# Routing attention and SwiGLU on one core: one-hot copies through GpSimd, q/k transposes held per head pair, a later second batch, feed-forward ahead of preparation

## The chip, the cores and the metric

The kernel runs on one core of one Trainium2 chip. The metric is device time in microseconds (us). A core has TensorE (PE: matmuls; PEld is its weight load), VectorE (DVE), ScalarE (ACT), GpSimd (POOL) and the DMA queues of SyncE (SP), ScalarE and GpSimd. Each engine works through its own instructions in the order in which they were written.

## The reference

Attention in which a query sees only the keys of its own cluster, then a gated feed-forward. Cut to what matters:

```python
# q, k, v: (4, 8, 768, 64); centroids: (8, 16, 64)
q_assign = argmax(q_n @ c_n); k_assign = argmax(k_n @ c_n)     # per head, normalised
mask = q_assign[:, :, :, None] == k_assign[:, :, None, :]
attn = softmax(where(mask, q @ k.T / 8, -1e9)); y = attn @ v
x = y as (3072, 512)
xn = x / sqrt(mean(x * x) + 1e-6) * rms_g
out = (silu(xn @ w_gate) * (xn @ w_val)) @ w_out               # 512 -> 1536 -> 512
```

## The kernel before

The 32 (batch, head) pairs, numbered n, form eight groups g of four heads. The mask is folded into the matmul: to the 64 rows of q and k that each head has come 16 rows of a one-hot of its cluster, so that the 80-row product of kext and qext holds the score plus a large term where the clusters agree; the exponential takes that term off again.

To prepare a group (`group_work`), each head's q and k, staged side by side by DMA, are transposed on TensorE in two parts (`trans`, tile tq), copied by ScalarE to `qkT`, cast by GpSimd into qext (`qcast`) and by VectorE into kext (`kcast`), and v is cast by GpSimd into vbf (`vcast`). Then `scores_c`, called with m = 0 and 1 for the two halves of the sequence, multiplies with the centroids (tile sc); VectorE transposes, takes the maximum, compares and transposes back (tile oh), and eight small DMAs, two for each head, copy the one-hot rows from oh into qext and kext. `qkT` is one tile of four heads, in a pool of one buffer (`qk32`).

The work runs in eight units u, each half the queries of one batch: unit 0 and 1 are batch 0 (groups 0 and 1), 2 and 3 batch 1 (groups 2 and 3), and so on. For each of the eight heads h of a unit three pairs of score matmuls go to TensorE (`scores`), each followed by one exponential on ScalarE (tile pT), and `pv` accumulates the head before against v (tile acc, one PSUM buffer for two heads; VectorE's reciprocal and multiplication into x free it). Between these pieces the unit gives out its `fill`, a list of (cost, function) pairs, so that the costs given out keep pace with the unit's 24 score steps (6 in unit 0). In unit u >= 2 the fill is the out matmuls of unit u - 2, then gate and value matmuls of unit u - 1 mixed with the preparation of a later group. `rms(u - 1)` stands after the second score step of unit u: ScalarE's last squares, a chain of VectorE's, the normalised tile xn. `ffn_work` transposes xn (tile tx, line 310) and then goes through the gate and val products, 12 of each.

What the change touches:
- The start (lines 395 to 418). `t0(h)` transposes head h of group 0. With `early` set, ScalarE also casts each half of k from PSUM into kext, and the eight one-hot DMAs of group 0 are triggered by ScalarE, each set of four once its oh is there. Group 1's first two heads follow. The 8 warm matmuls at the beginning have a tile in the pool of the scores, `ps_s`.
- Unit 0 (line 441). Its fill is the rest of group 1's preparation (`first[4:]`) and then the loads of all weights, which GpSimd triggers.
- `second_batch` (lines 428 to 433), called in unit 0 after the head before head 6 has been accumulated. A tiny DMA `hold` makes SP wait for the latest reciprocal of that unit; the loads of q, k and v of batch 1 stand behind it.
- Unit 1 (lines 443 and 444). Its fill begins with six pieces of group 2 (three heads' transposes) and then mixes `ffn_work(0)` with the rest of groups 2 and 3.
- `gv` (lines 329 to 332). Tanh goes to a tile th, and VectorE's (th + 1) * gate to a second tile gu.

Of the kernel before, what the change touches and what calls it, by code (L numbers as in the profile page):

```python
# [9 lines left out]
F32 = mybir.dt.float32  # L10
# [3 lines left out]
ALU = mybir.AluOpType  # L14
ACT = mybir.ActivationFunctionType
# [3 lines left out]
ZS = 2048.0  # L19
# [3 lines left out]
def kernel(  # L23
# [12 lines left out]
    nc = tc.nc  # L36
    B, H, S, D = q.shape
# [3 lines left out]
    P = 128  # L41
# [3 lines left out]
    HG = 4  # L45
# [10 lines left out]
    pool = lambda n, b, **kw: ctx.enter_context(tc.tile_pool(name=n, bufs=b, **kw))  # L56
    const = pool("const", 1)
    stage = pool("stage", NQ)
    qk32 = pool("qk32", 1)
    asg = pool("asg", 1)  # L60
    ptp = pool("ptp", 3)
    xp = pool("xp", 1)
# [14 lines left out]
    def load_qk(n, kq=None):  # L77
        if n >= B * H:
            return
        staged[n] = stage.tile([P, ST, 2, D], F32, tag="qk", name="qk")  # L80
        nc.sync.dma_start(out=staged[n][:, :, 0], in_=src(q, n))
        (kq or nc.sync).dma_start(out=staged[n][:, :, 1], in_=src(k, n))
# [17 lines left out]

    warm = const.tile([P, 512], BF16)
    nc.vector.memset(warm, 1.0)
    warm_ps = ps_s.tile([P, 2, 512], F32, tag="s", name="warm")
    for i in range(WARM):
        nc.tensor.matmul(warm_ps[:, i % 2], lhsT=warm[:, :P], rhs=warm, start=True, stop=True)


    def rsqrt(ms, n):
# [13 lines left out]
        return y  # L122


    ones = const.tile([P, P], F32)
    nc.vector.memset(ones, 1.0)
    cnt = const.tile([P, 32], F32)
    nc.vector.tensor_tensor_scan(cnt, ones[:, 0:32], ones[:, 0:32], 0.0, op0=ALU.mult, op1=ALU.add)
    cntT = const.tile([P, 32], F32)
    nc.vector.transpose(cntT, cnt)  # L130
    ident_f = const.tile([P, P], F32)
# [48 lines left out]

    qkT = {}

    def trans(g, h, part, early=False):
        if (h, part) == (0, 0):
            qkT[g] = qk32.tile([P, HG, S], F32, tag="qkT", name="qkT")
        qk = staged[g * HG + h]
        ps = ps_g.tile([P, UQ], F32, tag="gen", name="tq")
        for i in range(HT):
            t = part * HT + i
            nc.tensor.transpose(ps[:, i * P:(i + 1) * P], qk[:, t].rearrange("p a d -> p (a d)"), ident_f)  # L190
        c = slice(part * UQ, (part + 1) * UQ)
        nc.scalar.copy(qkT[g][:, h, c], ps)  # L192
        if early:
            nc.scalar.activation(kext[g % 4][:D, h, c], ps[D:], ACT.Copy, scale=1.0 / ZS)

    def qcast(g, h):
        nc.gpsimd.tensor_copy(qext[g % 4][:D, h], qkT[g][:D, h])  # L197

    def kcast(g, h):
        nc.vector.tensor_scalar_mul(kext[g % 4][:D, h], qkT[g][D:, h], 1.0 / ZS)  # L200

    def vcast(n):
        nc.gpsimd.tensor_copy(vbf[n // HG % 4][:, n % HG, :, :D], stagedv[n])
# [8 lines left out]
    def scores_c(g, m, h0=0, h1=HG, early=False):  # L212
        if not early:
            ps = ps_g.tile([P, UQ], F32, tag="gen", name="sc")
        else:
            if m == 0:
                scps[g, h0] = ps_s.tile([P, 2, 512], F32, tag="s", name="sc")
            ps = scps[g, h0][:, m, :UQ]
        r = slice(32 * h0, 32 * h1)
        for h in range(h0, h1):  # L220
            nc.tensor.matmul(ps[32 * h:32 * h + 32], lhsT=cblk[:, g * HG % H + h],  # L221
                             rhs=qkT[g][:, h, m * UQ:(m + 1) * UQ], start=True, stop=True)
# [12 lines left out]
        nc.vector.transpose(oh[r, m * UQ:(m + 1) * UQ], ohT[r])  # L235
        if m:
            for h in range(h0, h1):
                q_ = nc.scalar if early else nc.sync
                q_.dma_start(out=qext[g % 4][D:D + NC, h], in_=oh[32 * h:32 * h + NC])
                q_.dma_start(out=kext[g % 4][D:D + NC, h], in_=oh[32 * h + NC:32 * h + 2 * NC])  # L240

# [73 lines left out]
    def gv(u, f, val):  # L315
        if f == 0 and not val:
            gvT[u] = xp.tile([P, FC, UQ], BF16, tag="gvT", name="gvT")
        w = wv if val else wg
        ps = ps_g.tile([P, UQ], F32, tag="gen", name="val" if val else "gate")
        for c in range(CC):  # L320
            nc.tensor.matmul(ps, lhsT=w[:, c, f * P:(f + 1) * P], rhs=xnT[u][:, c], start=c == 0, stop=c == CC - 1)  # L321
        last = u == NU - 1
        if not val:
            th = ffn.tile([P, UQ], F32, tag="th", name="th")
            if last:
                nc.scalar.activation(th, ps, ACT.Silu)
                gates[u] = th
            else:
                nc.scalar.activation(th, ps, ACT.Tanh, scale=0.5)  # L329
                gu = ffn.tile([P, UQ], F32, tag="gu", name="gu")  # L330
                nc.vector.scalar_tensor_tensor(gu, th, 1.0, ps, op0=ALU.add, op1=ALU.mult)  # L331
                gates[u] = gu
        elif last:
            nc.vector.tensor_mul(gvT[u][:, f], gates[u], ps)
        else:
            nc.vector.scalar_tensor_tensor(gvT[u][:, f], gates[u], 0.5, ps, op0=ALU.mult, op1=ALU.mult)  # L336
# [16 lines left out]
    def group_work(g):  # L353
        w = []
        for h in range(HG):
            n = g * HG + h
            w.append((0.25, lambda h=h: trans(g, h, 0)))

            def second(h=h, n=n):
                trans(g, h, 1)  # L360
                qcast(g, h)
                kcast(g, h)
                vcast(n)
                if g > 1:
                    load_qk(n + NQ)
                    load_v(n + NV)
            w.append((0.25, second))
        for m in range(2):
            w.append((0.7, lambda m=m: scores_c(g, m)))
        return w  # L370
# [23 lines left out]

    def t0(h):
        for part in range(2):
            trans(0, h, part, True)
        qcast(0, h)
        if NQ + h < H:
            load_qk(NQ + h)  # L400

    first = group_work(1)
    t0(0)
    centroids_t()
    t0(1)
    for n in range(2, H):
        load_v(n)
    nc.sync.dma_start(out=gcol, in_=moe_rms_g.rearrange("(c p) -> p c", p=P), allow_slow_non_contiguous=True)
    t0(2)
    for m in range(2):  # L410
        scores_c(0, m, 0, 2, True)
    t0(3)
    for m in range(2):
        scores_c(0, m, 2, 4, True)
    for h in range(HG):
        vcast(h)
    for _, f in first[:4]:
        f()

    def weights():  # L420
        for c in range(CC):
# [78 lines left out]
```

## Time and profile before

| | |
|---|---|
| median of 3 runs | 405.89 us (405.69 to 407.38) |
| profiled execution, its own time | 405.33 us |
| its span, first to last instruction | 403.4 us |
| mean granted clock of TensorE | 0.941 |
| busy: PE, PEld | 359.1 us (89%), 217.5 us (54%) |
| busy: DVE, ACT, POOL | 241.7 us (60%), 260.3 us (65%), 57.5 us (14%) |

By stage, from the trace's windows:

| us from the span's start | PE busy | ACT busy | DVE busy | PE clock |
|---|---|---|---|---|
| 0 to 20 | 10.69 | 8.82 | 10.04 | 0.97 |
| 20 to 40 | 14.30 | 11.13 | 12.92 | 0.69 |
| 40 to 60 | 14.85 | 14.06 | 1.51 | 0.57 |
| 60 to 80 | 10.82 | 8.01 | 8.75 | 0.59 |
| 80 to 100 | 18.92 | 14.72 | 13.66 | 0.99 |
| 100 to 120 | 19.68 | 16.03 | 13.47 | 1.00 |

The busy share of an engine is a mean over stages with different limits; the granted clock is a share of TensorE's full speed, and a matmul at half clock takes about twice as long, so a busy TensorE at 0.57 does little more than half of what it does at 1.00. Unit 0 runs from about 29 to 60 us, unit 1 from there to about 113.

### The profile page before, as it was taken

Reading aid. Unit: us, or ns where it says so; the run is one execution under the profiler, and the core shown is the slowest. Engines: PE = TensorE matmul, PEld = TensorE weight load, DVE = VectorE, ACT = ScalarE, POOL = GpSimd, SP = SyncE. Lnnn points to the kernel's source line nnn. Section 1 sums busy time; section 2 is a strip of 40 time slices with the busy share of each in tenths; the row PEclk is TensorE's granted clock in tenths of the full one; section 3 lists DMA queues with packets and bytes.
Section 4 is the critical chain, followed back from the end, with each engine's and each line's share of the span. In section 5 each row is a group of like instructions: output and inputs, shape, how many; then the busy total and the mean of one; then the engine's idle time right before and its main releaser. Section 6 shows DMA issues by size and latency. Waiting matters only on the chain.

```text
span 403.4 us, 7758 instructions
## 1 busy us (share of the span) xinstructions
PE 359.1 (89%) x3003; PEld 217.5 (54%) x3017; DVE 241.7 (60%) x556; ACT 260.3 (65%) x459; POOL 57.5 (14%) x84
## 2 busy tenths in 40 slices
PE   6458685589999999999998999899999999999896
PEld 3135344357645665566555664566556655664452
DVE  5457001686677678766865677566876646666432
ACT  5329584368875877678766876577767785784230
POOL 1149203203300320022101220031100000000000
PEclk9958655699999999999999999999999999999999
DMA  9923999954512432224222100200020002000102
GB/s 171 243 77 66 215 199 254 265 121 108 128 32 89 98 80 63 91 66 117 61 70 69 41 2 17 82 2 0 3 83 18 0 2 80 0 2 26 53 1 80
DMA packets 63877, 32.01 MB, mean 79 GB/s; under 512 B 53088, under 2 KB 59744, under 8 KB 63840
## 3 DMA queue, kind: packets, MB, share of 16 engines
q1 hardware_dynamic: 57712, 25.80, 25.7%
q0 software_dynamic: 2736, 4.72, 6.5%
q10 hardware_dynamic: 3392, 0.98, 1.3%
q8 instruction: 24, 0.39, 0.4%
q14 instruction: 13, 0.11, 0.1%
HBM read 28.35 MB, written 6.29 MB: 86 GB/s over the span
## 4 chain that ended last, share of the span: by engine, by line
PE 69%; DVE 9%; ACT 9%; DMA 7%; issue 3%; ACTq 1%; SPq 1%; DVEq 0%
PE gate L321 15%; PE val L321 14%; PE s L253 13%; PE o L345 9%; PE acc L269 8%; PE tq L190 5%; ACT pT L255 4%; ACT junk L288 3%; DMA out_dram<-o_sb 3%; PE sc L221 3%; DMA qk<-in_q_dram 2%; DMA qk<-in_k_dram 2%; DVE o_sb L348 1%; DMA kext<-oh 1%; PE tx L310 1%
## 5 line engine op out<-in xcount | busy, mean ns | idle before, releaser
L255 ACT ACTIVATE pT<-s,off 128x768 bf16<-128x768 f32 x192 | 171.4, 901 | 57.7 <-PE s L253 57.5
L253 PE MATMUL s<-qext,kext 80*128 80x384 bf16 x384 | 98.8, 343 | 5.6 <-DMA kext<-oh 3.4
L321 PE MATMUL gate<-xnT,wg 128*128 128x384 bf16 x384 | 79.6, 327 | 1.1 <-ACT qkT L192 1.0
L321 PE MATMUL val<-xnT,wv 128*128 128x384 bf16 x384 | 78.1, 325 | 0.2 <-DVE gvT L336 0.2
L331 DVE SCALAR_TENSOR_TENSOR gu<-th,gate 128x384 f32<-128x384 f32 x84 | 46.3, 551 | 45.3 <-ACT th L329 44.8
L345 PE MATMUL o<-wo,gvT 128*128 128x512 bf16 x274 | 68.2, 379 | 0.8
L197 POOL CAST qext<-qkT 64x768 bf16<-64x768 f32 x32 | 32.5, 1015 | 222.4 <-ACT qkT L192 222.3
L253 PEld LDWEIGHTS <-kext 80*128 80x128 bf16 x384 | 37.0, 102 | 40.4 <-issue 15.3
L269 PEld LDWEIGHTS <-pT 128*128 128x128 bf16 x1152 | 48.7, 101 | 15.6 <-ACT pT L255 5.8
L269 PE MATMUL acc<-vbf,pT 128*128 128x65 bf16 x1152 | 52.5, 198 | 4.2 <-ACT pT L255 3.9
L336 DVE SCALAR_TENSOR_TENSOR gvT<-gu,val 128x384 bf16<-128x384 f32 x84 | 46.5, 554 | 10.5 <-PE val L321 3.7
L329 ACT ACTIVATE th<-gate 128x384 f32<-128x384 f32 x84 | 41.0, 488 | 17.1 <-PE gate L321 17.1
L192 ACT COPY qkT<-tq 128x384 f32<-128x384 f32 x64 | 30.2, 479 | 33.6 <-PE tq L190 18.8
L321 PEld LDWEIGHTS <-wg 128*128 128x128 bf16 x384 | 36.2, 98 | 24.1 <-issue 3.2
L321 PEld LDWEIGHTS <-wv 128*128 128x128 bf16 x384 | 36.2, 97 | 22.8 <-issue 0.6
L190 PE MATMUL tq<-ident_f,qk 128*128 128x128 f32 x192 | 35.4, 311 | 10.3 <-DMA qk<-in_k_dram 4.1
L345 PEld LDWEIGHTS <-gvT 128*128 128x128 bf16 x288 | 26.7, 97 | 27.1
L190 PEld LDWEIGHTS tq<-ident_f,qk 128*128 128x128 f32 x192 | 26.8, 161 | 20.3 <-ACT qkT L192 5.2
L200 DVE TENSOR_SCALAR kext<-qkT 64x768 bf16<-64x768 f32 x28 | 21.2, 758 | 15.8 <-ACT qkT L192 14.9
L348 DVE COPY o_sb<-o 128x512 f32<-128x512 f32 x24 | 15.9, 687 | 13.3 <-PE o L345 7.6
L274 DVE RECIPROCAL inv<-acc 128x6 f32<-128x6 f32 x32 | 6.0, 187 | 29.2 <-PE acc L269 29.1
L221 PE MATMUL sc<-qkT,cblk 128*32 128x384 f32 x128 | 17.5, 514 | 6.2 <-ACT qkT L192 4.8
(57 smaller groups left out, 206.1 us busy)
## 6 DMA issues: line engine op xcount, KB each, us to landing
qk<-in_q_dram SPq DMA_DIRECT2D x32, 192.0 KB, 4.2
vs<-in_v_dram SPq DMA_DIRECT2D x32, 192.0 KB, 3.6
out_dram<-o_sb SPq DMA_DIRECT2D x24, 256.0 KB, 2.1
qk<-in_k_dram SPq DMA_DIRECT2D x28, 192.0 KB, 4.4
wg<-in_moe_w_gate_dram POOLq DMA_DIRECT2D x4, 384.0 KB, 9.3
wv<-in_moe_w_val_dram POOLq DMA_DIRECT2D x4, 384.0 KB, 10.6
wo<-in_moe_w_out_dram POOLq DMA_DIRECT2D x3, 512.0 KB, 17.3
qk<-in_k_dram ACTq DMA_DIRECT2D x4, 192.0 KB, 5.4
```

The lines of the kernel that those rows point to most:

```text
L190: nc.tensor.transpose(ps[:, i * P:(i + 1) * P], qk[:, t].rearrange("p a d -> p (a d)"), ident_f)
L192: nc.scalar.copy(qkT[g][:, h, c], ps)
L197: nc.gpsimd.tensor_copy(qext[g % 4][:D, h], qkT[g][:D, h])
L221: nc.tensor.matmul(ps[32 * h:32 * h + 32], lhsT=cblk[:, g * HG % H + h], rhs=qkT[g][:, h, m * UQ:(m + 1) * UQ], start=True, stop=True)
L253: nc.tensor.matmul(ps[:, j, :UQ], lhsT=kext[g % 4][:KR, hh, kc * P:(kc + 1) * P], rhs=qext[g % 4][:KR, hh, hf * UQ:(hf + 1) * UQ], start=T ...
L255: nc.scalar.activation(pT[u, h][:, 2 * i:2 * i + 2], ps[:, :, :UQ], ACT.Exp, bias=off, scale=scale * ZS)
L269: nc.tensor.matmul(acc[:, h % 2, t], lhsT=pT[u, h][:, kc, t * P:(t + 1) * P], rhs=vbf[g % 4][:, hh, kc], start=kc == 0, stop=kc == ST - 1)
L321: nc.tensor.matmul(ps, lhsT=w[:, c, f * P:(f + 1) * P], rhs=xnT[u][:, c], start=c == 0, stop=c == CC - 1)
L329: nc.scalar.activation(th, ps, ACT.Tanh, scale=0.5)
L331: nc.vector.scalar_tensor_tensor(gu, th, 1.0, ps, op0=ALU.add, op1=ALU.mult)
L336: nc.vector.scalar_tensor_tensor(gvT[u][:, f], gates[u], 0.5, ps, op0=ALU.mult, op1=ALU.mult)
L345: nc.tensor.matmul(outs[u], lhsT=gvT[u][:, f, t * P:(t + 1) * P], rhs=wo[:, f], start=f == 0, stop=f == FC - 1)
```

## The change

Group 0's one-hot DMAs are triggered by GpSimd (`q_ = nc.gpsimd if early`). `qkT` becomes a tile of two heads with three buffers. ScalarE's cast of k into kext is one operation for a whole head, placed later. Group 1's kext casts are taken out of the heads' preparation and put behind both `scores_c` of that group. `clusters0`, `vcast` and group 1's first heads are put in another order; 2 and 6 further warm matmuls are added, and the warm tile moves to the pool of acc. `second_batch` is called in unit 1 at head 0. Unit 1's fill begins with an empty item of cost 3.0 and 12 feed-forward pieces; groups 2 and 3 are mixed with the remaining 16. (th + 1) * gate is written in place. `ones` shrinks to the 32 columns in use.

```diff
-    qk32 = pool("qk32", 1)
+    qk32 = pool("qk32", 3)
...
-    warm_ps = ps_s.tile([P, 2, 512], F32, tag="s", name="warm")
-    for i in range(WARM):
-        nc.tensor.matmul(warm_ps[:, i % 2], lhsT=warm[:, :P], rhs=warm, start=True, stop=True)
+    warm_ps = ps_a.tile([P, 512], F32, tag="acc", name="warm")
+
+    def busy(n):
+        for i in range(n):
+            nc.tensor.matmul(warm_ps, lhsT=warm[:, :P], rhs=warm, start=True, stop=True)
+
+    busy(WARM)
...
-    def trans(g, h, part, early=False):
-        if (h, part) == (0, 0):
-            qkT[g] = qk32.tile([P, HG, S], F32, tag="qkT", name="qkT")
+    def trans(g, h, part):
+        if (h % 2, part) == (0, 0):
+            qkT[g, h // 2] = qk32.tile([P, 2, S], F32, tag="qkT", name="qkT")
...
-        nc.scalar.copy(qkT[g][:, h, c], ps)
+        nc.scalar.copy(qkT[g, h // 2][:, h % 2, c], ps)
...
+    def kcast(g, h, early=False):
         if early:
-            nc.scalar.activation(kext[g % 4][:D, h, c], ps[D:], ACT.Copy, scale=1.0 / ZS)
...
+            nc.scalar.activation(kext[g % 4][:D, h], qkT[g, h // 2][D:, h % 2], ACT.Copy, scale=1.0 / ZS)
+            return
+        nc.vector.tensor_scalar_mul(kext[g % 4][:D, h], qkT[g, h // 2][D:, h % 2], 1.0 / ZS)
...
-                q_ = nc.scalar if early else nc.sync
+                q_ = nc.gpsimd if early else nc.sync
...
-                gu = ffn.tile([P, UQ], F32, tag="gu", name="gu")
-                nc.vector.scalar_tensor_tensor(gu, th, 1.0, ps, op0=ALU.add, op1=ALU.mult)
-                gates[u] = gu
+                nc.vector.scalar_tensor_tensor(th, th, 1.0, ps, op0=ALU.add, op1=ALU.mult)
+                gates[u] = th
...
                 qcast(g, h)
-                kcast(g, h)
                 vcast(n)
                 if g > 1:
+                    kcast(g, h)
...
     t0(0)
     centroids_t()
+    busy(2)
     t0(1)
+    kcast(0, 0, True)
...
     t0(2)
-    for m in range(2):
-        scores_c(0, m, 0, 2, True)
+    kcast(0, 1, True)
+    clusters0(0)
     t0(3)
-    for m in range(2):
-        scores_c(0, m, 2, 4, True)
-    for h in range(HG):
-        vcast(h)
-    for _, f in first[:4]:
+    kcast(0, 2, True)
+    vcast(0)
+    vcast(1)
+    for _, f in first[:2]:
         f()
+    kcast(0, 3, True)
+    clusters0(2)
+    vcast(2)
+    vcast(3)
+    for _, f in first[2:4]:
+        f()
+    busy(6)
...
-            fill = first[4:] + [(0.0, weights)]
+            fill = first[4:] + [(0.0, lambda h=h: kcast(1, h)) for h in range(HG)] + [(0.0, weights)]
         elif u == 1:
             prep = group_work(2) + group_work(3)
-            fill = prep[:6] + spread(ffn_work(0), prep[6:])
+            f0 = ffn_work(0)
+            fill = [(3.0, lambda: None)] + f0[:12] + spread(f0[12:], prep)
...
-                    if (u, h) == (0, H - 2):
+                    if (u, h) == (1, 0):
                         second_batch()
```

`clusters0(h)` is `scores_c(0, m, h, h + 2, True)` for m = 0 and 1.

How the instructions stand on the engines shows in three places. The first is the start, on ScalarE, from the last copies of head 2 of group 0 to the first exponential (qkT, kext, qext as above; L192 and L196 are the same copy). Before:

```order
L239 DMA qext_143<-oh 16x768
L240 DMA kext_147<-oh 16x768
L239 DMA qext_143<-oh 16x768
L240 DMA kext_147<-oh 16x768
L192 COPY qkT<-tq 128x384
L194 ACTIVATE kext_147<-tq 64x384
```

Now ScalarE triggers none of these, and GpSimd's row of the start reads:

```order
L199 CAST qext_143<-qkT 64x768 x3
L244 DMA qext_143<-oh 16x768
L245 DMA kext_147<-oh 16x768
L244 DMA qext_143<-oh 16x768
L245 DMA kext_147<-oh 16x768
L199 CAST qext_143<-qkT 64x768
L208 CAST vbf_151<-vs 128x6x64 x2
L199 CAST qext_144<-qkT 64x768
L208 CAST vbf_152<-vs 128x6x64
L244 DMA qext_143<-oh 16x768
L245 DMA kext_147<-oh 16x768
```

The triggers of the first two heads moved from between ScalarE's copies to behind three casts of GpSimd; those of heads 2 and 3 stand there behind five more casts, one of them of group 1's v.

The second place is VectorE at the end of group 1's preparation in unit 0 (oh is that group's last transpose, kext_148 its kext, inv and x the normalisation of the unit's first two heads). Now:

```order
L229 STREAM_TRANSPOSE scT<-sc 128x384
L233 TENSOR_REDUCE mx<-scT 128x24
L235 TENSOR_TENSOR ohT<-scT,mx 128x384
L240 STREAM_TRANSPOSE oh<-ohT 128x384
L205 TENSOR_SCALAR kext_148<-qkT 64x768 x4
L279 RECIPROCAL inv<-acc 128x6
L281 TENSOR_TENSOR x<-acc,inv 128x2x3x64
```

Before, the four casts to kext_148 stood ahead of both clusters chains, and the reciprocal came right behind the last oh; they moved to between the two.

The third place is ScalarE at the start of unit 1, from the last squares of unit 0's first three quarters (junk, 384 columns) on. Before:

```order
L255 ACTIVATE pT<-s,off 128x768
L192 COPY qkT<-tq 128x384 x4
L255 ACTIVATE pT<-s,off 128x768
L288 ACTIVATE junk,ss<-x 128x128 x3
L192 COPY qkT<-tq 128x384 x3
L255 ACTIVATE pT<-s,off 128x768
L192 COPY qkT<-tq 128x384
L329 ACTIVATE th<-gate 128x384
```

Now:

```order
L260 ACTIVATE pT<-s,off 128x768 x2
L293 ACTIVATE junk,ss<-x 128x128 x3
L260 ACTIVATE pT<-s,off 128x768 x2
L334 ACTIVATE th<-gate 128x384
L260 ACTIVATE pT<-s,off 128x768
```

The copies of group 2, four of which stood ahead of unit 0's last squares and four between these and the first th, are gone from there; the first of them now stands behind the fifth th.

More of the change, by code (lines that the diff above doesn't have):

```diff
@@ L122, in rsqrt @@
         return y
-    ones = const.tile([P, P], F32)
+    ones = const.tile([P, 32], F32)
     nc.vector.memset(ones, 1.0)
     cnt = const.tile([P, 32], F32)
-    nc.vector.tensor_tensor_scan(cnt, ones[:, 0:32], ones[:, 0:32], 0.0, op0=ALU.mult, op1=ALU.add)
+    nc.vector.tensor_tensor_scan(cnt, ones, ones, 0.0, op0=ALU.mult, op1=ALU.add)
     cntT = const.tile([P, 32], F32)
@@ L191, in trans, with qcast @@
         c = slice(part * UQ, (part + 1) * UQ)
-        nc.scalar.copy(qkT[g][:, h, c], ps)
+        nc.scalar.copy(qkT[g, h // 2][:, h % 2, c], ps)
+    def qcast(g, h):
+        nc.gpsimd.tensor_copy(qext[g % 4][:D, h], qkT[g, h // 2][:D, h % 2])
+    def kcast(g, h, early=False):
         if early:
-            nc.scalar.activation(kext[g % 4][:D, h, c], ps[D:], ACT.Copy, scale=1.0 / ZS)
[L196 to L200, printed above, removed]
+            nc.scalar.activation(kext[g % 4][:D, h], qkT[g, h // 2][D:, h % 2], ACT.Copy, scale=1.0 / ZS)
+            return
+        nc.vector.tensor_scalar_mul(kext[g % 4][:D, h], qkT[g, h // 2][D:, h % 2], 1.0 / ZS)
     def vcast(n):
@@ L221, in scores_c @@
             nc.tensor.matmul(ps[32 * h:32 * h + 32], lhsT=cblk[:, g * HG % H + h],
-                             rhs=qkT[g][:, h, m * UQ:(m + 1) * UQ], start=True, stop=True)
+                             rhs=qkT[g, h // 2][:, h % 2, m * UQ:(m + 1) * UQ], start=True, stop=True)
         sct = asg.tile([P, UQ], F32, tag="scT", name="scT", bufs=2)
@@ L396, in t0 @@
         for part in range(2):
-            trans(0, h, part, True)
+            trans(0, h, part)
         qcast(0, h)
@@ L400, in t0, with clusters0 @@
             load_qk(NQ + h)
+    def clusters0(h):
+        for m in range(2):
+            scores_c(0, m, h, h + 2, True)
     first = group_work(1)
```

## The prediction

> **What bounds the kernel now.** I read the page first, then TensorE's waits in the first 130 us, then windows by stage, then the timeline of the stages that lose time.
>
> ```profile
> span 403.4 us, 7758 instructions
> ```
>
> Up to 130 us TensorE's longest single waits are these (us in total, times, longest):
>
> ```profile
> PE sc L221 <- ACT qkT L192: 4.8, 1, 4.8
> PE tx L310 <- DVE xn L301: 4.6, 1, 4.6
> PE s L253 <- DMA kext<-oh: 3.4, 1, 3.4
> ```
>
> They make 12.8 us, all before 80 us, and the change touches each. The windows (length; busy us of PE, PEld, DVE, ACT and POOL with counts; then granted clock, DMA share and GB/s) show what follows from them:
>
> ```profile
> 39.40:42.80 3.40, 1.89 (x24) 1.10 (x23) 0.19 (x1) 3.16 (x5) 1.57 (x3) 0.99 1.04 197
> 43.00:44.00 1.00, 0.00 (x0) 0.00 (x0) 0.00 (x0) 0.11 (x1) 0.08 (x1) 0.50 1.06 209
> 46.00:60.00 14.00, 12.42 (x99) 7.00 (x96) 1.51 (x4) 11.19 (x16) 0.00 (x0) 0.50 1.15 205
> 75.00:80.30 5.30, 5.08 (x25) 3.41 (x26) 3.28 (x8) 1.93 (x4) 0.81 (x1) 0.50 1.22 273
> 81.00:115.20 34.20, 32.92 (x324) 20.73 (x321) 24.07 (x47) 26.72 (x47) 6.84 (x9) 1.00 0.44 108
> ```
>
> The second half of unit 0 runs at half the clock (0.50), and from 81 us TensorE is the bound: 32.92 of 34.2 us busy at full clock. From the first out matmul on (115.19, below) the same work follows in the same order in both kernels, but for gu, which is now written into th's tile by an operation of the same shape; I cost that at nothing, since VectorE, which does it, is not the bound there. So the forecast is how much earlier that out matmul starts. Four marks lead to it: first exponential, last one of unit 0, first transpose of unit 1's feed-forward (tx), first out matmul.
>
> **A. To the first exponential.** The start's timeline (start us, us, engine; idle time before and its end in brackets):
>
> ```profile
> 15.20 0.57 DVE L235 STREAM_TRANSPOSE oh<-ohT 64x384 bf16<-64x384 bf16 x1
> ...
> 18.39 0.48 ACT L192 COPY qkT<-tq 128x384 f32<-128x384 f32 x1 [6.23 <-issue]
> ...
> 24.83 0.57 DVE L235 STREAM_TRANSPOSE oh<-ohT 64x384 bf16<-64x384 bf16 x1
> ...
> 27.98 1.24 ACT L192 COPY qkT<-tq 128x384 f32<-128x384 f32 x3 [7.58 <-DMA kext<-oh]
> ...
> 30.09 0.90 ACT L255 ACTIVATE pT<-s,off 128x768 bf16<-128x768 f32 x1 [0.16 <-PE s L253]
> ```
>
> ScalarE's queue holds the eight one-hot DMAs of group 0, and each set of four waits for VectorE's last transpose (15.77, then 25.40). Until then the copies behind them, which heads 2 and 3 and then all of group 1 need, stand still: 6.23 and 7.58 us. With the DMAs on GpSimd and qkT in three tiles of two heads, ScalarE's copies follow the loads. Heads 2 and 3 are then copied while VectorE is at the first clusters chain, and the second chain follows it directly: eight operations of about 0.57 us from 15.77 end near 20.4 instead of 25.4. What decides the first scores is then the one-hot of head 0.
>
> ```profile
> kext<-oh ACTq DMA_DIRECT2D x4, 24.0 KB, 2.7
> DMA to landing us min/median/max: 1.8/1.9/6.0
> L175 POOL DMA_DIRECT2D wv<-in_moe_w_val_dram x4: 551/566/588, 36.0 to 39.2; - x4
> DMA to landing us min/median/max: 6.0/10.6/14.8
> ```
>
> No one-hot goes through GpSimd in this trace. A trigger there takes 0.57 us for the wide wv; landing is bounded by 1.8 us (quickest one-hot from any queue) and by 6.0 (quickest wv, 16 times the bytes). ScalarE's own took 2.7 under the same loads; I take 3.3, near it, since the size is the same. The second trigger (kext of head 0) goes at 16.4 and lands at 19.7. TensorE gets there near 19.8 (an estimate: the second chain's scores may start after its first transpose, 16.4, and take 0.8; six transposes 1.1 by the row in part D; six warm matmuls 1.5): these fill a gap in which it would wait anyway, and cost nothing. ScalarE's added 768-wide casts (0.90 us each by the exponential's row below) lie in its former idle time. First exponential about 0.8 us after landing: 20.5 instead of 30.09, **-9.6 us**; bounds -9.8 (TensorE is no earlier) and -6.9 (landing 6.0).
>
> The other four triggers wait for 20.4 and for casts ahead of them that need v's loads; with two triggers and 3.3 they land near 26. Cover: the two heads before, six exponentials and four copies, 7.3 us, which puts head 2's scores near 27.
>
> **B. From the first exponential to the last of unit 0.**
>
> ```profile
> L255 ACT ACTIVATE pT<-s,off 128x768 bf16<-128x768 f32 x192 | 171.4, 901 | 57.7 <-PE s L253 57.5
> L200 DVE TENSOR_SCALAR kext<-qkT 64x768 bf16<-64x768 f32 x28 | 21.2, 758 | 15.8 <-ACT qkT L192 14.9
> 28.87 0.56 DVE L200 TENSOR_SCALAR kext<-qkT 64x768 bf16<-64x768 f32 x1 [3.46 <-ACT qkT L192]
> 31.88 1.42 DVE L200 TENSOR_SCALAR kext<-qkT 64x768 bf16<-64x768 f32 x1 [1.35 <-ACT qkT L192]
> 38.34 0.58 DVE L235 STREAM_TRANSPOSE oh<-ohT 128x384 bf16<-128x384 bf16 x1
> 39.03 0.56 DVE L276 TENSOR_TENSOR x<-acc,inv 128x384 f32<-128x384 f32 x1
> 40.44 0.62 PE L269 MATMUL acc<-vbf,pT 128*128 128x65 bf16 x14 [0.18 <-ACT pT L255]
> 45.11 0.82 PE L253 MATMUL s<-qext,kext 80*128 80x384 bf16 x2 [3.40 <-DMA kext<-oh]
> 46.03 0.90 ACT L255 ACTIVATE pT<-s,off 128x768 bf16<-128x768 f32 x1 [2.92 <-PE s L253]
> 49.49 0.90 ACT L255 ACTIVATE pT<-s,off 128x768 bf16<-128x768 f32 x1 [0.20 <-PE s L253]
> 52.96 0.90 ACT L255 ACTIVATE pT<-s,off 128x768 bf16<-128x768 f32 x1 [0.20 <-PE s L253]
> 59.30 0.89 ACT L255 ACTIVATE pT<-s,off 128x768 bf16<-128x768 f32 x1
> ```
>
> Before, this takes 60.19 - 30.09 = 30.1 us. The wait for group 1's one-hots (2.92 us of ScalarE) goes: they are now issued about when the weights start, not behind six DMAs of weights. In its place comes a **new wait**. The four kext casts of group 1 now stand on VectorE behind the second clusters chain and ahead of the reciprocal that frees the only acc tile. Before, that chain ended at 38.92 and acc was free at 39.59. Now it is free four casts later: 3.0 us at the mean of 0.758; 2.2 if each takes 0.56, 5.7 if each takes 1.42. The accumulation of head 2 could go at 40.44 - 30.09 = 10.35 us after the first exponential; now at 8.83 + 0.67 + 3.0 = 12.5. I count **+2.3** with what hangs behind it (1.5 to 5.0). Behind the stalled accumulation stand the next scores, so ScalarE starves too. The clock then falls about where it fell before, and heads 4 to 6 keep the slow pitch (52.96 - 49.49 = 3.47 us). B: -2.9 + 2.3 = **-0.6**.
>
> The 1.42 beside GpSimd's work bears on a rule of the Trainium skill, "SBUF — State Buffer", section "Who interferes with whom": VectorE and GpSimd share a port pair, a tensor_scalar may take it whole, and whoever comes second stands still. The weights' descriptors are written on GpSimd just then; by the rule alone all four casts could take 1.42, and the sum would be 2.7 us later. The mean row stands against that, so I keep 0.758.
>
> **C. From there to tx.**
>
> ```profile
> 54.74 0.61 SPq L81 DMA_DIRECT2D qk<-in_q_dram  x1
> 60.08 0.52 ACT L288 ACTIVATE junk<-x 128x384 bf16<-128x384 f32 x1
> 64.33 1.51 PE L190 MATMUL tq<-ident_f,qk 128*128 128x128 f32 x6 [3.14 <-DMA qk<-in_k_dram]
> 69.64 0.30 ACT L288 ACTIVATE junk<-x 128x128 bf16<-128x128 f32 x1
> 74.95 1.40 PE L310 MATMUL tx<-ident,xn 128*128 128x128 bf16 x6 [4.61 <-DVE xn L301]
> 115.19 0.38 PE L345 MATMUL o<-wo,gvT 128*128 128x512 bf16 x1
> ```
>
> Before: 74.95 - 60.19 = 14.76 us, because group 2's transposes stand ahead of the rms and wait for loads that came 9.6 us after issue. Now nothing of group 2 stands there. ScalarE does the rest of a square sum (about 0.7), two exponentials (1.8) and the last squares; from these to tx it was 74.95 - 69.64 = 5.31. Sum 7.8: **-6.95**. TensorE has no work of its own there and waits some 5 us; the added empty item of 3.0 only puts that wait where ScalarE needs it. The loads now start after unit 0's last reciprocal, near 51.5, land near 61 by the same 9.6, and are asked for by group 2 some 11 us after tx, near 69 (four transposes and eight gate or val products come first, partly at half clock). Cover 7 us; a load later than that costs its delay in full. The gate weights were issued until 39.2 and landed 14.8 us later at worst, 24 us after the first exponential; even 5 us later they precede tx, 37 us after it.
>
> **D. From tx to the first out matmul.** 115.19 - 74.95 = 40.24 us before.
>
> ```profile
> L190 PE MATMUL tq<-ident_f,qk 128*128 128x128 f32 x192 | 35.4, 311 | 10.3 <-DMA qk<-in_k_dram 4.1
> L253 PE MATMUL s<-qext,kext 80*128 80x384 bf16 x384 | 98.8, 343 | 5.6 <-DMA kext<-oh 3.4
> L192 ACT COPY qkT<-tq 128x384 f32<-128x384 f32 x64 | 30.2, 479 | 33.6 <-PE tq L190 18.8
> L329 ACT ACTIVATE th<-gate 128x384 f32<-128x384 f32 x84 | 41.0, 488 | 17.1 <-PE gate L321 17.1
> ```
>
> Work comes back: 18 transposes that were done by then (18 x 35.4/192 = 3.3 us) less one scores pair already done (0.5): +2.8. All 16 copies, 16 exponentials and 8 th now share the last two thirds of the unit: 7.7 + 14.4 + 3.9 + 2.1 of squares = 28.1 us of ScalarE, about TensorE's own work there. If TensorE stays 96% busy as in 81 to 115, crowding costs nothing; if ScalarE can only be 26.72/34.2 = 78% busy, it takes 36 us, +7. I take +2, nearer the first, since TensorE set the pace in that row. The start at half clock is paid in both. D: **+4.8**.
>
> **Sum.** -9.6 - 0.6 - 6.95 + 4.8 = -12.35. The profiled execution took 405.33 us (span 403.4); the forecast is 393.0. The median of the runs, 405.89, lies 0.56 above the profiled one, far less than the bounds.
>
> **Rivals.**
> 1. *The clock holds in unit 0.* Then heads 4 to 6 run at three exponentials, 2.7 us, instead of 3.47: 2.3 us less, 391. For: the first half of the unit runs at full clock. Against: in 39.40:42.80 TensorE was 1.89 of 3.4 us busy, and in 43:44 the clock is 0.50; the new wait leaves no more. The Trainium skill, "TensorE: Matmul & The Clock Gate", section "What's actually happening", has the clock fall after at least one idle window of about 3.4 us. TensorE stood still only since 45.11 - 3.40 = 41.71, so the trace speaks against that rule as a length of idle time; by the rule alone this rival would be the forecast.
> 2. *One-hots through GpSimd land late*, 6.0 us after the trigger: 2.7 later in A, 395.7. For: a queue that the trace shows with large transfers only. Against: the size, 24 KB.
> 3. *ScalarE bounds the end of unit 1*: +5 on D, 398.
> 4. *Slower than before: the clock stays halved through unit 1.* From tx TensorE has some 38 us of full-clock work (32.92, half of 5.08, and the 2.8 of D); at 0.50 that is 76 instead of 45, near 424. Each us spent cold costs half a us, so it decides from 25 us more of it. For: the row 46:60 stayed at 0.50 for 14 us with TensorE 89% busy. Against: 75 to 80.3, 96% busy on the same feed-forward work, brought it back.
> 5. *The feed-forward is not what delayed unit 1, the xn chain is later for another reason*, so C gives nothing: 400.
>
> **How the numbers follow.** Forecast 0.50, rivals in order 0.22, 0.12, 0.08, 0.04, 0.04. The range 387 to 399 takes in rivals 1 to 3 and the bounds of A, B and D taken together, not all at their ends at once. A change of under 0.5% (2 us) is about what a measurement of this kernel cannot tell from none. Faster by more 0.94, within 0.02, slower 0.04: rival 4 alone is slower, and rivals 3 and 5 would have to come together to eat the gain.
>
> **What would show it.** A: first exponential near 20.5, no ScalarE wait over 2 us before it. B: TensorE or VectorE waiting about 2 us at the third head's accumulation, kext casts just before it; no wait for kext<-oh over 1 us. C: tx about 8 us after the last exponential of unit 0, no transpose waiting for qk loads. D: 45 us from tx to the first out matmul, ScalarE over 85% in its last 20 us. It would be wrong if one-hots land after 23 us, if the clock is 0.50 past tx + 8, or if the marks after the first out matmul shift.

## The result, and the profile after

| | before | changed |
|---|---|---|
| median of the runs on one chip | 406.49 us (405.69 to 407.38, 4 runs) | 389.64 us (388.49 to 392.3, 4 runs) |
| profiled execution, its span | 405.33, 403.4 us | 389.09, 387.2 us |
| mean granted clock | 0.941 | 0.955 |

The ratio is 0.959, 95% interval 0.954 to 0.965: faster. Ratios here and below are taken from runs no more than 1.5% above the fastest of their kernel; among the changed kernels this leaves out only two of x8's six. The profiled execution came out 16.2 us shorter, where 12.35 was forecast. TensorE's longest waits of the changed kernel up to 130 us (us in total, times, longest), against those shown of before:

```profile
PE tx L315 <- DVE xn L306: 4.6, 1, 4.6
PE s L258 <- DMA kext<-oh: 2.6, 2, 1.4
...
PE acc L274 <- DVE x L281: 2.1, 1, 2.1
```

The 4.8 us wait for ScalarE's copies is gone, the one for xn stands as it was, and the forecast new wait of the accumulation for x is there. The four marks, read from the timelines of the profiled executions (us from the span's start), with the three best later kernels beside them:

| | first exp | last exp of unit 0 ends | tx | first out matmul | span |
|---|---|---|---|---|---|
| before | 30.09 | 60.19 | 74.95 | 115.19 | 403.4 |
| changed | 20.72 | 51.21 | 58.10 | 99.08 | 387.2 |
| x10_onehots_first | 20.74 | 47.87 | 54.76 | 96.20 | 382.4 |
| x11_and_warm | 21.30 | 48.44 | 55.32 | 95.20 | 381.8 |
| x12_unit0_filled | 20.96 | 46.33 | 52.72 | 92.61 | 377.4 |

The differences between the marks are the terms of the sum (us):

| term | before | changed | difference | forecast |
|---|---|---|---|---|
| A, to the first exponential | 30.09 | 20.72 | -9.37 | -9.6 |
| B, to the last of unit 0 | 30.10 | 30.49 | +0.39 | -0.6 |
| C, to tx | 14.76 | 6.89 | -7.87 | -6.95 |
| D, to the first out matmul | 40.24 | 40.98 | +0.74 | +4.8 |
| the rest | 288.21 | 288.12 | -0.09 | 0 |

From the changed kernel's timeline of the start and of unit 0 (start us, us, engine; idle time before it and its end in brackets):

```profile
16.12 0.52 POOL L245 DMA_DIRECT2D kext<-oh  x1
18.68 1.81 DVE L235 TENSOR_TENSOR ohT<-scT,mx 64x384 bf16<-64x384 f32 x1
20.18 0.50 PE L258 MATMUL s<-qext,kext 80*128 80x384 bf16 x2 [1.39 <-DMA kext<-oh]
20.72 0.90 ACT L260 ACTIVATE pT<-s,off 128x768 bf16<-128x768 f32 x1 [2.65 <-PE s L258]
28.94 0.58 DVE L240 STREAM_TRANSPOSE oh<-ohT 128x384 bf16<-128x384 bf16 x1
29.55 2.21 DVE L205 TENSOR_SCALAR kext<-qkT 64x768 bf16<-64x768 f32 x4
30.82 0.56 POOL L179 DMA_DIRECT2D wv<-in_moe_w_val_dram  x1
31.89 0.56 DVE L281 TENSOR_TENSOR x<-acc,inv 128x384 f32<-128x384 f32 x1
32.51 1.17 PE L274 MATMUL acc<-vbf,pT 128*128 128x65 bf16 x18 [2.12 <-DVE x L281]
34.36 1.69 ACT L260 ACTIVATE pT<-s,off 128x768 bf16<-128x768 f32 x2 [2.93 <-PE s L258]
36.13 0.82 PE L258 MATMUL s<-qext,kext 80*128 80x384 bf16 x2 [1.17 <-DMA kext<-oh]
50.32 0.89 ACT L260 ACTIVATE pT<-s,off 128x768 bf16<-128x768 f32 x1
53.69 0.30 ACT L293 ACTIVATE junk<-x 128x128 bf16<-128x128 f32 x1
58.10 1.40 PE L315 MATMUL tx<-ident,xn 128*128 128x128 bf16 x6 [4.60 <-DVE xn L306]
```

The scores start once head 0's one-hot has landed; the four casts (29.55 to 31.76) stand between the last oh and the x that frees acc; and 6.89 us after the last exponential (50.32 + 0.89) comes tx. The median landing of the four one-hots written into kext, from the DMA view of the first 90 us, and the windows of the stages (columns as in the prediction):

```profile
kext<-oh POOLq DMA_DIRECT2D x4, 24.0 KB, 2.8
```

```profile
27.92:31.33 3.41, 1.76 (x20) 0.94 (x20) 3.31 (x7) 3.16 (x4) 3.41 (x7) 1.00 0.54 85
31.00:32.00 1.00, 0.00 (x0) 0.00 (x0) 0.97 (x4) 0.43 (x1) 1.00 (x3) 0.66 1.15 209
32.00:33.00 1.00, 0.49 (x10) 0.50 (x11) 0.45 (x1) 0.00 (x0) 0.44 (x1) 0.50 1.02 175
46.00:51.00 5.00, 4.24 (x31) 2.39 (x30) 0.00 (x0) 4.63 (x9) 0.00 (x0) 0.50 1.21 199
58.63:62.05 3.42, 3.31 (x33) 2.64 (x33) 1.51 (x5) 0.90 (x1) 0.00 (x0) 0.50 1.01 265
58.10:62.00 3.90, 3.68 (x34) 2.81 (x35) 1.99 (x6) 0.90 (x1) 0.00 (x0) 0.50 1.00 261
62.00:99.08 37.08, 35.76 (x344) 23.16 (x343) 26.77 (x50) 29.92 (x55) 13.13 (x16) 1.00 0.64 157
79.08:99.08 20.00, 18.70 (x189) 11.43 (x190) 15.86 (x29) 16.06 (x32) 8.54 (x11) 1.00 0.52 134
```

The clock falls at 31.33, just under 1 us after TensorE began to wait for x (its last scores end at 30.38); the mean of 0.66 from 31 to 32 gives the same moment. It stays at 0.50 to the end of unit 0 and comes back at 62.05, 3.9 us after tx. In the last 20 us of D TensorE is 94% busy and ScalarE 80%.

That the rest came out equal may be in part luck. From 359.0 to 362.4 us the clock of the changed kernel's profiled execution was at 0.50, which happens nowhere in the rest of the one before; in the traces of x1 to x12 the rest takes 284.8 to 290.6 us.

### The profile page after: what moved, and what is told of

Its sections match the earlier page's. It is cut to its first block, busy times and chain, and to the rows that moved or that the text cites. A ratio compares the mean times of both kernels' runs of the same rounds, so it can differ in the third digit from the quotient of the medians.

```text
span 387.2 us, 7799 instructions
## 1 busy us (share of the span) xinstructions
PE 356.9 (92%) x3010; PEld 215.1 (56%) x3025; DVE 241.8 (62%) x556; ACT 258.1 (67%) x455; POOL 60.4 (16%) x92
## 4 chain that ended last, share of the span: by engine, by line
PE 73%; DVE 9%; ACT 8%; DMA 5%; issue 3%; POOL 0%; SPq 0%; DVEq 0%; ACTq 0%
PE gate L326 16%; PE val L326 15%; PE s L258 14%; PE o L349 10%; PE acc L274 9%; PE tq L194 5%; ACT pT L260 4%; ACT junk L293 3%; DMA kext<-oh 3%; PE sc L226 2%; DMA out_dram<-o_sb 2%; PE tx L315 1%; DVE o_sb L352 1%; DVE oh L240 1%; PE warm L107 1%
## 5 line engine op out<-in xcount | busy, mean ns | idle before, releaser
L326 PE MATMUL val<-xnT,wv 128*128 128x384 bf16 x384 | 79.1, 329 | 0.0
L335 DVE SCALAR_TENSOR_TENSOR th<-th,gate 128x384 f32<-128x384 f32 x84 | 46.3, 551 | 45.7 <-ACT th L334 45.1
L199 POOL CAST qext<-qkT 64x768 bf16<-64x768 f32 x32 | 30.9, 967 | 196.8 <-ACT qkT L196 196.8
L340 DVE SCALAR_TENSOR_TENSOR gvT<-th,val 128x384 bf16<-128x384 f32 x84 | 46.5, 553 | 9.6 <-PE val L326 3.6
L196 ACT COPY qkT<-tq 128x384 f32<-128x384 f32 x64 | 29.8, 482 | 11.2 <-PE tq L194 10.2
L194 PE MATMUL tq<-ident_f,qk 128*128 128x128 f32 x192 | 31.5, 282 | 1.3 <-DVE gvT L340 0.6
L194 PEld LDWEIGHTS tq<-ident_f,qk 128*128 128x128 f32 x192 | 23.2, 143 | 10.7 <-DVE gvT L340 2.7
L293 ACT ACTIVATE junk<-x 128x384 bf16<-128x384 f32 (+1 forms) x48 | 20.1, 418 | 2.5 <-DVE x L281 2.0
```

The lines of the kernel that those rows point to most:

```text
L196: nc.scalar.copy(qkT[g, h // 2][:, h % 2, c], ps)
L199: nc.gpsimd.tensor_copy(qext[g % 4][:D, h], qkT[g, h // 2][:D, h % 2])
L293: nc.scalar.activation(junk[:, c], xs[u][:, t, c], ACT.Square, accum_out=sq[u][:, int(last), t:t + 1])
L335: nc.vector.scalar_tensor_tensor(th, th, 1.0, ps, op0=ALU.add, op1=ALU.mult)
```

## The experiments

Each kernel was compared with the kernel before on its own chip, where that one's medians lay between 405.13 and 405.76 us; x9 to x11 ran on one chip, the others of x1 to x12 on another. Times are medians with lowest and highest, ratios are to the kernel before with 95% intervals. All start from the changed kernel unless said otherwise.

### The one-hots' queue (A)

x1 puts the one-hot triggers of group 0 back on ScalarE; x2 is the kernel before with these alone moved to GpSimd.

```diff
-                q_ = nc.gpsimd if early else nc.sync
+                q_ = nc.scalar if early else nc.sync
```

> The changed kernel with group 0's one-hot DMAs back on ScalarE's queue, nothing else undone. Theory (the start is won because ScalarE's queue no longer waits for one-hots): the copies of head 3 and of group 1 stand behind the triggers again, first exponential near 30 instead of 20.7, time near 398.5. Rival (the start is won by qkT in three tiles, which lets group 1's copies go before group 0's cluster scores are done): first exponential within 3 us of 20.7, time under 392.

> The kernel before with one word changed: group 0's one-hot DMAs triggered by GpSimd. Theory: first exponential near 21 and nearly the whole 9.4 us of the start, time near 396.5 (profiled 405.3 before), although qkT is still one tile. Rival (the three tiles are needed as well): copies of group 1 wait for the second cluster scores and for casts, first exponential 24 or later, time over 400.

x1: 396.97 us (395.55 to 400.2), ratio 0.980 [0.974, 0.986], 7.3 above the changed kernel. Its timeline shows the two stalls of before again, behind the triggers:

```profile
18.25 0.86 ACT L196 COPY qkT<-tq 128x384 f32<-128x384 f32 x2 [6.71 <-issue]
28.42 0.86 ACT L196 COPY qkT<-tq 128x384 f32<-128x384 f32 x2 [7.10 <-DMA kext<-oh]
29.31 0.90 ACT L260 ACTIVATE pT<-s,off 128x768 bf16<-128x768 f32 x1
```

x2: 400.76 us (399.14 to 402.68), ratio 0.988 [0.983, 0.994], less of a gain than expected: the time is the rival's. Its first exponential comes at 22.44, between the two, and these rows of its timelines show what stands in the way:

```profile
19.68 1.63 ACT L192 COPY qkT<-tq 128x384 f32<-128x384 f32 x4 [4.50 <-POOL qext L197]
...
36.10 1.17 PE L269 MATMUL acc<-vbf,pT 128*128 128x65 bf16 x18 [3.38 <-DVE x L276]
```

With one qkT tile for four heads in a pool of one buffer, group 1's copies wait until GpSimd has cast the last q of group 0, group 1's preparation comes later, and the accumulation waits longer for x than in the changed kernel (3.38 us against 2.12). The queue alone brings most of the earlier first exponential, but what it brings is kept only with the other edits; the three smaller qkT tiles and the new order were not tried apart.

### Order of unit 1 and place of the loads (C)

x3 writes unit 1's list as before (loads still in unit 1), x4 puts the loads back into unit 0 (list as changed), x5 does both.

```diff
-            f0 = ffn_work(0)
-            fill = [(3.0, lambda: None)] + f0[:12] + spread(f0[12:], prep)
+            fill = prep[:6] + spread(ffn_work(0), prep[6:])
...
-                    if (u, h) == (1, 0):
+                    if (u, h) == (0, H - 2):
```

> The changed kernel with unit 1's list as before (six pieces of group 2 first), the second batch's loads still in unit 1. Theory (group 2's transposes ahead of the rms wait for loads that have only just been issued): TensorE waits again for qk loads, tx 4 to 6 us later than 58.1, less 2 us of transposes done by then; time 392 to 394. Rival (tx is set by the xn chain whatever stands ahead): tx within 1 us of 58.1, time under 390.

> The changed kernel with the second batch's loads back in unit 0 behind head 5, unit 1's list as changed. Theory (the order of the list alone matters, since the feed-forward asks for no load): time within 1.5 us of 389.6. Rival (the loads of before delay weights or the one-hots of group 1, so that holding them back is what pays): time 392 or more, with a wait for wg, wv or for kext<-oh over 1 us longer than the changed kernel has.

> The changed kernel with both unit 1's list and the second batch's loads as before. Theory (the list's order is worth 7 us when the loads come early, as in the kernel before, and the loads' place alone is worth nothing): last exponential of unit 0 to tx 14 to 15 us instead of 6.9, work behind tx shorter by 1; time 395 to 397.5, 1 to 2 us less than with the order alone undone. Rival (holding the loads back is worth something of its own): 398 or more.

x3: 397.92 us (395.91 to 399.54), 0.981 [0.975, 0.988]; x4: 388.36 (387.16 to 388.61), 0.957 [0.953, 0.961]; x5: 395.84 (395.74 to 397.55), 0.977 [0.972, 0.982]. The transposes of x3, from its timeline:

```profile
58.04 1.51 PE L194 MATMUL tq<-ident_f,qk 128*128 128x128 f32 x6 [5.04 <-DMA qk<-in_k_dram]
60.98 1.51 PE L194 MATMUL tq<-ident_f,qk 128*128 128x128 f32 x6 [1.43 <-DMA qk<-in_k_dram]
...
69.27 0.69 PE L315 MATMUL tx<-ident,xn 128*128 128x128 bf16 x2 [4.50 <-DVE xn L306]
```

In x3 tx comes 17.28 us after the last exponential, in x5 15.75, in x4 6.89 as in the changed kernel. So the order accounts for all of C (x5 against x4: 7.5 us of the time), and holding the loads back is worth nothing that can be told here; with the old order tx even comes 1.5 us later, since group 2's transposes ask for the loads sooner than they come. x3 came out above its expectation because tx comes 11.2 us later than in the changed kernel, where 4 to 6 were expected: its C is even 2.5 us longer than that of the kernel before.

### The two waits of unit 0 (B)

x6 issues group 1's kext casts with their heads' preparation, ahead of its cluster chains. x7 is x6 with group 1's first two heads' one-hots triggered by GpSimd ahead of the weights. x9 puts the casts behind the reciprocal and x of heads 0 and 1 instead; x10 is x9 with the same one-hots on GpSimd. The edits of x9 and x10 (in all four kernels the casts leave the fill; the change of `q_` is not in x6 and x9):

```diff
-            fill = first[4:] + [(0.0, lambda h=h: kcast(1, h)) for h in range(HG)] + [(0.0, weights)]
+            fill = first[4:] + [(0.0, weights)]
...
+                    if (u, h) == (0, 2):
+                        for k_ in range(HG):
+                            kcast(1, k_)
...
-                q_ = nc.gpsimd if early else nc.sync
+                q_ = nc.gpsimd if early or (g == 1 and h < 2) else nc.sync
```

> The changed kernel with group 1's four kext casts moved ahead of its cluster scores, two behind group 0's second chain and two in the heads' own preparation. Theory (the casts cause the wait of the accumulation for x, 2.1 us of TensorE, but the one-hots of head 4, which land near 36, wait next): no wait for x over 0.5 us, the wait for kext<-oh grows from 1.2 to about 3 us, time within 1.5 us of 389.6. Rival (the casts' wait is worth what ScalarE idles there, 2.9 us): 387 or less.

> The run before, and the one-hots of group 1's first two heads triggered by GpSimd ahead of the weights. Theory (with both waits gone TensorE is some 70% busy through unit 0 and the clock holds): granted clock 1.00 from 30 us to the end of unit 0, heads 4 to 6 at about 2.8 us instead of 3.47, last exponential of unit 0 near 46 instead of 51.2, time 382.5 to 385.5. Rival 1 (the clock falls all the same at that load): 0.50 from about 35, time 385.5 to 388. Rival 2 (weights issued 3 us later arrive after tx): a wait for wg or wv of over 1 us behind tx.

> The changed kernel with group 1's four kext casts moved behind the reciprocal and x of heads 0 and 1, so that they no longer hold the acc tile. Theory (casts make the wait for x, but head 4's one-hot, which lands near 36, is the next thing late): TensorE's wait of acc for x near 32 us goes from 2.1 to under 0.5, the wait of head 4's scores for kext<-oh grows from 1.2 to about 3, and the time stays within 1.5 of the changed kernel's 389.6. Rival (the 2.9 us that ScalarE idled at the accumulation are lost for good): 387 or less.

> The kernel before it with the one-hot DMAs of group 1's first two heads triggered by GpSimd too, ahead of the weights. Both waits go: no wait of TensorE for x or kext<-oh over 1 us between the first and the last exponential of unit 0, head 4's scores near 33 us instead of 36. If the clock falls because of these waits it holds at 1.00 through unit 0, each head takes about 2.8 us, and the time is 382.5 to 384.5. Rival (the clock falls anyway at that load, TensorE 70 to 80% busy): the row of 40 to 50 us shows 0.50, and the time is 385.5 to 387.

x6: 390.08 us (388.36 to 391.61), 0.962 [0.957, 0.967]. The time is as expected, but the wait for x didn't go: 1.75 us of it stayed, and the wait for head 4's one-hot grew from 1.17 to 4.16. From its timeline:

```profile
24.49 2.27 DVE L205 TENSOR_SCALAR kext<-qkT 64x768 bf16<-64x768 f32 x1 [0.95 <-ACT qkT L196]
25.00 0.83 POOL L199 CAST qext<-qkT 64x768 bf16<-64x768 f32 x1
...
31.36 0.58 DVE L240 STREAM_TRANSPOSE oh<-ohT 128x384 bf16<-128x384 bf16 x1
```

A cast that took 0.55 us in the changed kernel, beside GpSimd's triggers, took 2.27 here beside GpSimd's own casts, and the chain ended 2.4 us later (31.94 instead of 29.52). x7: 386.45 (384.35 to 387.34), 0.952 [0.948, 0.957]: head 4 no longer waits for its one-hot, 1.7 us for x remain, and the clock falls all the same, as rival 1 had it.

x9: 388.83 (388.08 to 393.81), 0.961 [0.956, 0.966]: no gain, as the theory had it. The wait for x is gone, and the one behind it grew from 1.17 to 4.08:

```profile
36.59 0.80 PE L258 MATMUL s<-qext,kext 80*128 80x384 bf16 x2 [4.08 <-DMA kext<-oh]
37.48 0.90 ACT L260 ACTIVATE pT<-s,off 128x768 bf16<-128x768 f32 x1 [3.57 <-PE s L258]
```

x10: 385.76 (383.75 to 389.35), 0.951 [0.946, 0.956]: both waits are gone, and head 4's scores start at 32.66 instead of 36.13. The clock fell nevertheless, at 32.3, so the rival held. The windows of x10:

```profile
25.50:28.90 3.40, 2.86 (x35) 1.48 (x34) 3.26 (x6) 2.92 (x4) 2.73 (x4) 1.00 0.01 2
28.90:32.30 3.40, 2.26 (x27) 1.12 (x24) 3.21 (x8) 3.08 (x4) 2.48 (x5) 1.00 0.18 43
32.30:35.70 3.40, 3.04 (x24) 1.80 (x24) 0.75 (x2) 2.57 (x4) 3.40 (x8) 0.50 0.83 140
40.00:50.00 10.00, 8.97 (x72) 5.18 (x70) 1.51 (x4) 8.37 (x15) 0.74 (x1) 0.50 1.07 203
```

There is no TensorE wait over 0.7 us in the second of these rows, but TensorE is only 2.26 of 3.4 us busy: ScalarE sets the pace of a head (three exponentials), and at full clock TensorE's own work does not fill it.

### Work for TensorE while it waits

x8 is x7, and x11 is x10, with 14 added matmuls, whose result nobody reads, while TensorE waits for xn ahead of tx. Their operands are the tile `warm`, which holds ones, not zeros as the expectations have it. x12 adds one such matmul behind each score step of unit 0's heads 2 to 7, and makes the 14 to 18.

```diff
+    def busy_g(n):
+        ps = ps_g.tile([P, 512], F32, tag="gen", name="warm_g")
+        for i in range(n):
+            nc.tensor.matmul(ps, lhsT=warm[:, :P], rhs=warm, start=True, stop=True)
...
-            fill = [(3.0, lambda: None)] + f0[:12] + spread(f0[12:], prep)
+            fill = [(3.0, lambda: None), (0.0, lambda: busy_g(18))] + f0[:12] + spread(f0[12:], prep)
...
+                if u == 0 and h >= 2:
+                    busy_g(1)
```

> The run before, and 14 matmuls of 512 columns on a scratch tile ahead of tx, where TensorE waits about 4.6 us for xn. Theory (a full window there gives the feed-forward the full clock from tx on, and half clock after tx costs 2 us now): granted clock 1.00 within 1 us of tx, the way from tx to the first out matmul 39 to 40 us instead of 41, time 1 to 2 us below the run before. Rival (the clock's window does not fill, or the matmuls outlast the wait): no gain, tx later by up to 1.5 us.

> The kernel before it with 14 matmuls of 512 columns on zeros while TensorE waits for the xn chain ahead of tx. If the start of unit 1 costs because it runs at half clock, the clock is 1.00 from tx on and the time is 2 to 3 us less than without them (380 to 383). Rival (the clock was held already, or these matmuls outlast the wait): no gain, or up to 2 us more.

> The kernel before it with one matmul of 512 columns on zeros behind each score step of unit 0's heads 2 to 7, and 18 in place of 14 ahead of tx. Theory (in unit 0 the clock falls because TensorE's own work fills only 66 to 84% of 3.4 us there, with no wait over 0.7 us): filled to about 90%, the clock stays at 1.00 from 32 to 48 us, a head of unit 0 takes about 2.8 us instead of 3.6, the last exponential of unit 0 ends 3 to 4 us earlier after the first, and the time is 378 to 380. Rival (the clock falls at that place whatever TensorE does): 0.50 from 33 us on, and the added matmuls at half clock make the heads longer, 383 to 387.

x8: 383.4 us (379.57 to 385.6), 0.941 [0.935, 0.947]; its D is 39.88 against x7's 40.98, as expected. x11: 382.48 (380.97 to 383.7), 0.941 [0.937, 0.945]. x12: 379.35 (379.22 to 383.02), 0.937 [0.931, 0.942], the lowest median of all, 10.3 us below the changed kernel's. The windows of D of x10 and x11, then two of x12, and x12's mean clock:

```profile
54.76:96.20 41.44, 39.91 (x376) 26.17 (x377) 28.77 (x55) 30.86 (x56) 13.13 (x16) 0.94 0.84 197
```

```profile
55.32:95.20 39.88, 38.21 (x376) 24.84 (x377) 28.76 (x55) 30.84 (x56) 13.13 (x16) 1.00 0.83 201
```

```profile
40.00:50.00 10.00, 8.23 (x80) 4.70 (x83) 1.83 (x6) 9.48 (x21) 0.74 (x1) 1.00 1.08 207
45.47:48.89 3.42, 2.34 (x27) 1.37 (x27) 0.75 (x2) 3.39 (x9) 0.00 (x0) 1.00 1.06 209
```

```profile
core 0: 377.4 us, clock 0.999
```

With a warm start D is 1.56 us shorter for the same 376 matmuls. In x12 the clock does not fall in unit 0 at all: a head takes 2.95 us instead of 3.46 (by the starts of its exponentials), B is 25.37 instead of x11's 27.14, C 6.39 instead of 6.88. TensorE was 82 to 87% busy in each 3.41 us from 28.41 to 45.47, not quite the 90% expected. So the fall in unit 0 follows from how little TensorE had to do there, not from its waits alone. The medians of x11 and x12 are 3.1 us apart, but they ran on two chips, their ranges touch and the intervals of their ratios overlap. The marks and the clock carry this reading, not the medians alone: all six runs of x12 have a mean clock of 0.990 to 0.999, x11's six 0.967 to 0.978. Some 1.8 us of the difference of their spans lie behind the first out matmul, where x11's clock was at 0.50 from 353.9 to 357.4 us and x12's was not (half of such a stretch, 1.7 us, is what it costs by an estimate); nothing here shows that the filling of unit 0 did that.

## Why the prediction came out as it did

**A: right, and for its reasons.** x1 brings back both ScalarE stalls and 7.3 us of the time. The size is partly luck. The copy that decides, head 0's into kext, was triggered at 16.12, not 16.4, and its scores started 4.06 us later at 20.18, where 3.3 were taken for the landing; the exponential came 0.54 behind the scores, not 0.8 behind the landing. The median landing of the four, 2.8 us, hides this. Still 4.06 is well short of 6.0, which settles rival 2. The prediction's list of TensorE's longest single waits leaves out one of 3.81 us at 28.51, longer than its third: group 1's transposes, held up by the same ScalarE copies, so A loses nothing by it. What the prediction lumped together, x2 takes apart: GpSimd's queue alone moves the first exponential by 7.65 of the 9.37 us, but only some 5 us reach the end.

**B: the mechanism right, sum off by 1.0, with the other sign.** The new wait for x is there (TensorE 2.12, ScalarE 2.93 us), the casts were shorter than reckoned (2.21 us for four, not 3.0). Two steps failed. The step that group 1's one-hots would no longer wait: at SyncE's pace of some 0.6 us a trigger, with 5.2 us to landing at the median of that queue, head 4 still waited 1.17 (ScalarE 1.00). And the clock did not fall "about where it fell before": it fell 10.6 us after the first exponential, early in the new wait, against some 12.7 before, so that more of unit 0 ran at half clock. The new wait is not needed for that fall, since in x10, without it, the clock fell 11.6 us after the first exponential. x9 shows why the wait for x was not worth removing alone: the one for the one-hot stands directly behind it.

**C: right, 0.9 too small.** The order accounts for it (x3, x5). The 0.9 is the chain from the last squares to tx, 4.41 us here and 5.31 in the row of before that was used: in before two of its small VectorE operations took 0.81 and 0.42 us, in the changed kernel each took 0.16. No transpose waited for a load.

**D: the mis-sized term.** Forecast +4.8, measured +0.74. The groups of transposes in D, changed and before:

```profile
L194 PE MATMUL tq<-ident_f,qk 128*128 128x128 f32 x48 | 7.7, 276 | 0.6 <-DVE gvT L340 0.6
L258 PE MATMUL s<-qext,kext 80*128 80x384 bf16 x44 | 11.2, 336 | 0.0
```

```profile
L190 PE MATMUL tq<-ident_f,qk 128*128 128x128 f32 x30 | 5.6, 302 | 0.0
L253 PE MATMUL s<-qext,kext 80*128 80x384 bf16 x46 | 11.8, 338 | 0.0
```

With the 18 added transposes the group is 2.1 us longer, not 3.3: the mean of the profile's page was over all stages, with the half-clock ones of unit 0 in it. All 48 of the changed kernel ran at full clock, while of the 30 before six ran at half clock and took 1.7 of the 5.6 us. The scores are 0.6 less, as reckoned. The +2 for crowding of ScalarE was nothing: TensorE's idle time in D is 40.98 - 39.44 = 1.54 us, before it was 1.49 (38.75 busy of 40.24). ScalarE was 80% busy in the last 20 us, not over 85%. Crowding and transposes make 3.2 of the 4.1 us by which D was forecast too slow. And the clock came back 3.9 us after tx, not 5.35, which saves half of the 1.4 us, some 0.7; a part of that is in the transposes' row already, so some of the 4.1 stays unexplained. That the clock came back so soon is luck: between kernels with the same code from tx on it took from 3.8 us (x7, D 40.98) to 6.5 us (x4, D 42.24). The errors of the other terms (+0.2, +1.0, -0.9) nearly cancel, which is luck too, so the sum was too slow by about D's error.

**Rivals.** 1, the clock holds in unit 0: it did not, and x10 shows that it would not have with both waits removed either; with filling it holds (x12) and is worth 1.8 us in B, where the rival had 2.3. By the rule of the Trainium skill named there ("TensorE: Matmul & The Clock Gate", section "What's actually happening") a fall takes an idle window of about 3.4 us; in x10 the clock fell without any such idle time, so the trace speaks against it if idle means without work. 3 is refuted by D's row, 4 by the return of the clock at 62.0, 5 by x3 and x5.

## What to carry to other kernels

Price each instruction that changes its stage at the clock of the stage it moves into, not at the mean of the profile's page, and ask whether the new neighbour's engine really waits before charging for crowding. Before removing a wait, look for the one directly behind it: here the removal of the wait for x alone was worth nothing (x9), and that of both some 3 to 4 us (x10). Most of this came with the one-hots: x7, where 1.7 us for x stayed, gained 3.6 over x6, and x10 3.1 over x9; the one-hots alone, with the casts left in place, were not tried. And in a stage where ScalarE sets the pace, a TensorE that is a third idle may lose its clock, and matmuls without a use in its gaps can then be cheaper than the half clock.

## What the runs showed of the hardware

- In all 14 traces each stretch between two changes of the clock is a whole multiple of 3.41 us long: in the changed kernel from 31.33 to 62.05, nine of them; before from 42.76 to 70.06, eight; in x10 from 32.30 to 59.61, eight. So the clock is judged at fixed points, 3.41 us apart within one execution, and where they lie against the program differs from trace to trace.
- In the stretches between these points TensorE's busy share in the profile went with the clock as follows. The clock came back 24 times, each time after 0.94 or more (0.97 from 58.63 to 62.05 in the changed kernel), and never after 0.90 or less; so the 8.97 of 10 us in x10, 40 to 50, did not bring it back. It fell after at most 0.67 (x10, 28.89 to 32.30, with no wait over 0.7 us), and not once after more. Below that the busy share alone doesn't decide: some stretches of 0.43 to 0.67 kept the clock. Every stretch of x12 from 21.58 to 48.89 lies above 0.67, the lowest at 0.68 (45.47 to 48.89).
- VectorE's 64x768 cast took 0.55 us beside GpSimd's DMA triggers and up to 2.27 beside GpSimd's casts (x6); ohT, with both inputs in SBUF, took 1.81 at 18.68 beside GpSimd's casts and, in the same shape, 0.56 at 16.42 beside its triggers (the changed kernel). By the Trainium skill ("SBUF — State Buffer", section "Who interferes with whom") such operations share a port pair with GpSimd; these rows agree where GpSimd computes and show no stall where it writes descriptors.
- A 24 KB copy from GpSimd's queue cost 0.48 to 0.64 us to trigger and landed in 2.8 at the median of four, the first into kext in 4.0, against a median of 2.7 from ScalarE's queue in the kernel before.
